# Scores of a sliding-window attention on half blocks: 32 queries by 96 keys in eight parts of the PE array

## The chip, the cores and the metric

One core of a Trainium2 chip runs the kernel. The metric is the device time of one execution in microseconds. Three runs of the kernel before gave 360.49, 361.76 and 361.85 us; the median, 361.76 us, is the time before. PE is the matrix engine (its matmuls; PEld is its weight loads), DVE the vector engine, ACT the scalar engine, POOL the general engine, and SP's queue issues the transfers.

## The reference

A causal attention with a window of 64 positions, then a gated feed-forward layer. Eight batches, eight heads, 576 positions, 64 features a head; all in 32-bit floats.

```python
scores = scale * np.matmul(q, k.transpose(0, 1, 3, 2))
rel = pos[:, None] - pos[None, :]
mask = (rel >= 0) & (rel < window)          # window = 64
scores = np.where(mask, scores, -1000000000.0)
attn = np.exp(scores - np.max(scores, axis=-1, keepdims=True))
attn = attn / (np.sum(attn, axis=-1, keepdims=True) + 1e-09)
x = np.matmul(attn, v)                       # heads side by side: (8, 576, 512)
for k in range(5):                           # gate_pre: a causal convolution of five taps
    gate_pre += conv_w[k][None, None, :] * xp[:, k:k + S, :]
gate = 1.0 / (1.0 + np.exp(-gate_pre))
out = (gate * (x @ w_val)) @ w_out
```

The two weights and the convolution's words come as 64-bit floats and are split on the chip into two 32-bit parts.

## The kernel before, in words

**Attention.** The 576 positions of a head are 9 blocks of 64 queries. A block needs 128 keys: its own 64 and the 64 before it. Heads go in pairs (tile index hh, 0 or 1; a pair has 128 features on the partitions, 64 each), which makes 32 pairs and 288 blocks. Blocks are worked off in 36 groups m of eight blocks. A group has one score tile per head in PSUM, 128 partitions by 4 by 128 keys: four times two blocks on top of each other. The steps of a group, with the names that the code gives them:

- S(m), L433: 16 products, 64 queries by 128 keys each, on quarters of the array (64 rows by 64 columns: the head chooses the rows, the place of the block in the tile the columns). A product of 32-bit floats is two matmuls in the trace, so a group has 32.
- M(m,hh), L452: on DVE, four operations that add a mask tile and take the row minimum of the negated scores (`nm`); X(m,hh), L464: on ACT, four exponentials that also sum (`su`).
- Ra, Rb (L469 POOL, L474 DVE): the sums and their reciprocals `rc`. N(m,hh): the product with them, on POOL as one operation (L486) or on ACT as four (L484).
- PT(m,hh), L493: four transposes on PE into one PSUM bank (tile `pt`, one buffer); EP, L201: ACT copies them out (`pts`).
- AV(i), L516: for a pair i, 18 products with the values into PSUM (tile `av`).
- XH, XL: the result is split into a rounded part `xh` and a rest `xl` (ACT or DVE, then DVE).

**Convolution.** Five taps of a pair. The letter of the pair in `conv` chooses the way: K means taps as products with diagonal matrices `dg` on PE (L574, tile `g`, from a copy `x` of the result, step EX) and a copy out of PSUM (CC); P, and every pair behind the string, means one tap on ACT (L607) and four on DVE (L609). Before, three pairs of batch 0 went by PE. SIG, L804, is the sigmoid of a batch on ACT; batch 0's was in two pieces (`gate`), and each return from sigmoid to exponential loads a table.

**Feed-forward.** Per batch eight V pieces of 12 matmuls (L647, 288 columns), then HF on DVE (product with the gate), HH on ACT and HL on POOL (its split into `h_hi` and `h_lo`), and output tiles O of 12 matmuls (L713, 512 columns), EO (copy out) and a store.

**What sets the order.** Nothing is moved by hand. Each step is an `Op` with a cost per engine, what it depends on, what buffers it takes and frees, and a priority (`prio` plus the offset of its kind in `off`). `in_order` is a list planner: it plays the program through with these costs, and at each point takes for each engine the ready step that can start first. What comes out is written to each engine's queue in that order, and every engine runs its queue strictly in order. V, O and HF carry a large priority number (`ffn_prio`), so that they fill in where attention cannot go on. In the first microseconds, where PE would wait, the loop at the end puts spare products of the identity (L827) into PE's queue, as many as the planned gap holds.

The array has three shapes: whole (V, O, PT, taps), quarters (S) and halves by columns (AV). The planner charges `drain` for a change between them.

## Time and profile before

| | |
|---|---|
| median of three runs | 361.76 us (360.49 to 361.85) |
| profiled execution | 361.33 us, its span 359.5 us |
| PE busy | 351.7 us, 3994 matmuls |
| ACT busy | 286.9 us |
| DVE busy | 257.4 us |
| POOL busy | 129.3 us |
| transfers | 52.08 MB, 145 GB/s in the mean |
| granted PE clock | full in all slices |

The busy time of PE is a union over matmuls that overlap, and their ends are modelled, so it tells that something of PE is under way and not how full the array is. Lengths of pieces in the chain of waits are from the start of a piece to the start of what follows it there, and can be added. A group's busy time counts overlapping instructions once, its mean is that of one.

### The profile page before, as it was taken

Reading aid. Unit: us, or ns where it says so; the run is one execution under the profiler, and the core shown is the slowest. Engines: PE = TensorE matmul, PEld = TensorE weight load, DVE = VectorE, ACT = ScalarE, POOL = GpSimd, SP = SyncE. Lnnn points to the kernel's source line nnn. Section 1 sums busy time; section 2 is a strip of 40 time slices with the busy share of each in tenths; the row PEclk is TensorE's granted clock in tenths of the full one; section 3 lists DMA queues with packets and bytes.
Section 4 is the critical chain, followed back from the end, with each engine's and each line's share of the span. In section 5 each row is a group of like instructions: output and inputs, shape, how many; then the busy total and the mean of one; then the engine's idle time right before and its main releaser. Section 6 shows DMA issues by size and latency. Waiting matters only on the chain.

```text
span 359.5 us, 10642 instructions
## 1 busy us (share of the span) xinstructions
PE 351.7 (98%) x3994; PEld 310.1 (86%) x3994; DVE 257.4 (72%) x927; ACT 286.9 (80%) x929; POOL 129.3 (36%) x197
## 2 busy tenths in 40 slices
PE   8999999989999999999999999999999999999996
PEld 7888778978899878998899888997899888988985
DVE  4999999997587588887788866786888773672300
ACT  2988999999999999997999988998899854333222
POOL 7141545373145622451244612443244400330510
PEclk9999999999999999999999999999999999999999
DMA  8984474254573335445544455345422241002012
GB/s 275 397 328 133 142 234 130 95 198 162 193 228 133 100 125 190 133 133 176 180 162 133 134 190 192 123 146 173 143 62 84 86 150 66 0 32 88 2 58 88
DMA packets 22291, 52.08 MB, mean 145 GB/s; under 512 B 2656, under 2 KB 4960, under 8 KB 22240
## 3 DMA queue, kind: packets, MB, share of 16 engines
q1 hardware_dynamic: 22240, 51.41, 42.4%
q8 instruction: 31, 0.51, 0.6%
q14 instruction: 20, 0.16, 0.1%
HBM read 41.96 MB, written 9.44 MB: 143 GB/s over the span
## 4 chain that ended last, share of the span: by engine, by line
PE 69%; ACT 18%; DVE 9%; DMA 1%; issue 1%; POOL 0%; DVEq 0%; ACTq 0%
PE o L713 26%; PE v L647 20%; ACT p L464 8%; PE av L516 8%; PE s L433 6%; PE pt L493 6%; DVE gp L609 3%; PE g L574 3%; DVE p L452 2%; ACT pts L201 2%; ACT p L484 1%; ACT h_hi L201 1%; ACT gp L607 1%; ACT L464 1%; DMA st<-in_w_val_dram 1%
## 5 line engine op out<-in xcount | busy, mean ns | idle before, releaser
L464 ACT ACTIVATE p<-p,nm 128x128 f32<-128x128 f32 x288 | 112.5, 399 | 2.3 <-DVE nm L452 2.1
L609 DVE SCALAR_TENSOR_TENSOR gp<-av,cw,gp 128x575 f32<-128x575 f32 (+1 forms) x116 | 94.1, 811 | 7.8 <-ACT gp L607 6.5
L676 POOL TENSOR_TENSOR h_lo<-hf,h_hi 128x288 fp32r<-128x288 f32 (+2 forms) x80 | 53.7, 683 | 99.4 <-ACT h_hi L201 98.3
L647 PE MATMUL v<-xl,wv_hi 128*128 128x288 f32 x256 | 78.6, 307 | 0.0
L647 PE MATMUL v<-xh,wv_hi 128*128 128x288 f32 x256 | 75.4, 295 | 0.0
L647 PE MATMUL v<-xh,wv_lo 128*128 128x288 f32 x256 | 75.4, 295 | 0.0
L452 DVE CUSTOM_DVE_ANT_0 p<-s,mask 128x128 f32<-128x128 f32 x288 | 65.2, 284 | 12.7 <-PE s L433 12.0
L713 PE MATMUL o<-wo_hi,h_lo 128*128 128x512 f32 (+1 forms) x148 | 60.2, 406 | 1.1 <-POOL h_lo L676 1.1
L713 PE MATMUL o<-wo_lo,h_hi 128*128 128x512 f32 (+1 forms) x148 | 57.8, 391 | 0.0
L486 POOL TENSOR_TENSOR p<-p,rc 128x512 f32<-128x512 f32 x49 | 51.4, 1061 | 17.8 <-DVE rc L474 16.5
L713 PE MATMUL o<-wo_hi,h_hi 128*128 128x512 f32 (+1 forms) x148 | 57.5, 389 | 0.0
L464 ACT ACTIVATION_READ_ACCUMULATOR p<-p,nm 128x1 f32 x288 | 56.6, 196 | 0.0
L647 PEld LDWEIGHTS v<-xl,wv_hi 128*128 128x128 f32 x256 | 48.1, 188 | 2.1 <-issue 1.7
L647 PEld LDWEIGHTS v<-xh,wv_hi 128*128 128x128 f32 x256 | 48.2, 188 | 0.1
L647 PEld LDWEIGHTS v<-xh,wv_lo 128*128 128x128 f32 x256 | 48.1, 188 | 0.0
L493 PE MATMUL pt<-ident,p 128*128 128x128 f32 x288 | 44.2, 276 | 1.8 <-ACT pts L201 1.6
L201 ACT CAST h_hi<-hf 128x288 fp32r<-128x288 f32 (+2 forms) x80 | 28.5, 383 | 19.0 <-DVE hf L658 18.8
L469 POOL TENSOR_SCALAR su<-su 128x8 f32<-128x8 f32 x36 | 9.9, 275 | 93.8 <-ACT p L464 93.6
L201 ACT COPY pts<-pt 128x512 f32<-128x512 f32 x72 | 41.9, 583 | 1.8 <-PE pt L493 1.5
L658 DVE TENSOR_TENSOR hf<-v,gp 128x288 f32<-128x288 f32 x64 | 29.0, 454 | 19.1 <-PE v L647 18.3
L516 PEld LDWEIGHTS av<-pts,v 128*64 128x64 f32 x1152 | 36.2, 138 | 6.4 <-issue 3.5
L493 PEld LDWEIGHTS pt<-ident,p 128*128 128x128 f32 x288 | 33.8, 140 | 8.4 <-issue 3.1
(122 smaller groups left out, 506.8 us busy)
## 6 DMA issues: line engine op xcount, KB each, us to landing
v<-in_vw_dram SPq DMA_DIRECT2D x32, 576.0 KB, 4.2
out_dram<-ot SPq DMA_DIRECT2D x35, 256.0 KB, 2.0
qtb<-in_qT_dram SPq DMA_DIRECT2D x31, 288.0 KB, 4.4
ktb<-in_kT_dram SPq DMA_DIRECT2D x31, 288.0 KB, 4.6
st<-in_w_val_dram SPq DMA_DIRECT2D x4, 512.0 KB, 7.6
st<-in_w_out_dram SPq DMA_DIRECT2D x2, 1024.0 KB, 10.0
qtb<-in_qT_dram SPq DMA_DIRECT2D x1, 256.0 KB, 3.7
ktb<-in_kT_dram SPq DMA_DIRECT2D x1, 256.0 KB, 5.0
```

What stands on the lines that cost most here:

```text
L201: nc.scalar.copy(out=out, in_=in_)
L433: nc.tensor.matmul(sp_t[m, hh][half * W:half * W + W, t, :], lhsT=held("qt", i)[r, j * W:j * W + W], rhs=held("kt", i)[r, j * W:j * W + P] ...
L452: nc.vector.tensor_tensor_reduce(out=pe[:, t, :], in0=sp_t[u][:, t, :], in1=mk[first], scale=-SCALE, scalar=3.0e38, op0=ALU.add, op1=ALU.m ...
L464: nc.scalar.activation(out=pe[:, t, :], in_=pe[:, t, :], func=AF.Exp, scale=-1.0, bias=nm[:, t:t + 1], accum_out=su[:, t:t + 1])
L486: MUL[e](out=pe, in0=pe, in1=rc.unsqueeze(2).broadcast_to([P, GB, P]))
L493: nc.tensor.transpose(out=tp[:, t, :], in_=pe[:, t, :], identity=ident)
L516: nc.tensor.matmul(ap[hh * D:(hh + 1) * D, j * W:(j + 1) * W], lhsT=v_t[i][:, hh * NB + j, :], rhs=pts_t[m, hh][:, t, half * W:(half + 1) ...
L609: nc.vector.scalar_tensor_tensor(out=acc, in0=x, scalar=col, in1=acc, op0=ALU.mult, op1=ALU.add)
L647: nc.tensor.matmul(vp_t[u][:, 0:NH], lhsT=w[:, c, js], rhs=x[:, c, hs], start=(a + z == 0), stop=(a + z == NM - 1))
L658: nc.vector.tensor_mul(out=hf, in0=vp_t.pop(u)[:, 0:NH], in1=gp_t[b][:, jb, hs])
L676: SUB[e](out=h_lo[:, jb, dst:dst + hi - lo], in0=hf_t[u][:, lo:hi], in1=h_hi[:, jb, dst:dst + hi - lo].bitcast(F32))
L713: nc.tensor.matmul(op_t[key][:, 0:cs.stop - cs.start], lhsT=h[:, jb, col:col + P], rhs=w[:, jb, cs], start=(a + z == 0), stop=(a + z == NM ...
```

## The change

Scores are taken on half blocks: 32 queries need only 96 keys, so a group has 32 products of 32 queries by 96 keys. They lie on eight parts of the array, 64 rows by 32 columns (`tile_position`); four blocks stand on top of each other in a score tile, and the four positions along it are two blocks by two halves. Mask, row minimum and exponential work on 96 columns; nine mask tiles of 96 columns replace three of 128. The probabilities lie at the first 96 columns for first halves and at the last 96 for second halves of eight fixed tiles `pb`, whose other 32 columns are set to zero once, so that transposes and AV keep their shape. AV reads the 64 queries of a block as two runs of 32.

Around it: pair 1 leaves the way by PE (`conv` KKKP becomes KPKP), each tap on PE is a step of its own that the planner can place, the first step of the weights' split may go to ACT as an absolute value, N may go to DVE, batch 0's sigmoid is one piece, v has two buffers and hf four, the planner chooses by rank among the steps that can start within `look` of the first, and single steps have offsets of their own (`adj`). Spares are written into a free bank of the taps once such a bank was used.

```diff
...
-    sb={'p': 8, 'pts': 6, 'v': 3, 'qt': 3, 'kt': 3, 'ot': 2, 'hf': 3, 'w': 2, 'x': 2},
+    sb={'p': 8, 'pts': 6, 'v': 2, 'qt': 3, 'kt': 3, 'ot': 2, 'hf': 4, 'w': 2, 'x': 2},
-    flex=dict(EP='A', EO='AV', HH='A', XH='AV', HL='G', CC='AV', N='GA', EX='AV', WR='GV', DG='V'),
+    flex=dict(EP='A', EO='AV', HH='A', XH='AV', HL='G', CC='AV', N='GVA', EX='A', WR='GV', DG='GV', WH='AV'),
-    gate={0: (0, 2, 4)},
+    gate={},
-    conv='KKKP',
+    conv='KPKP',
+    adj={'PT(6, 1)': -7.65, 'PT(4, 1)': -2.76, 'EP(1, 1)': -0.17, 'X(6, 1)': -1.73,
...
+    look={'A': 100, 'P': 0, 'G': 450, 'V': 0},
...
                     continue
                 k = (t - (CFG["wait"] if e == "P" and op.prio < CFG["ffn_prio"] else 0)
                      - (CFG["stay"] if e == "P" and "F" != mode and op.mode != "F" else 0), op.rank)
-                if pick is None or k < pick[0]:
-                    pick = (k, op)
+                cand.append((k, op))
+            if cand:
+                limit = min(k for k, _ in cand)[0] + CFG["look"].get(e, 0)
+                pick = min((c_ for c_ in cand if c_[0][0] <= limit), key=lambda c_: c_[0][1])
             if pick and (best is None or pick[0] < best[0]):
                 best = (pick[0], e, pick[1])
         if best is None:
...
+    Q, KW = W // 2, W + W // 2
     mk = {}
...
+    def mask(where_):
+        m32 = const.tile([P, KW], F32, name="mask" if where_ is None else "mask%d%d" % where_)
+        if where_ is None:
+            nc.gpsimd.memset(m32, 0.0)
+            for c in range(4):
+                r = slice(c * Q, c * Q + Q)
+                nc.gpsimd.affine_select(
+                    out=m32[r], in_=m32[r], pattern=[[1, KW]], compare_op=ALU.is_ge,
+                    fill=NEG / SCALE, base=-1, channel_multiplier=-1)
+                nc.gpsimd.affine_select(
+                    out=m32[r], in_=m32[r], pattern=[[-1, KW]], compare_op=ALU.is_ge,
+                    fill=NEG / SCALE, base=W, channel_multiplier=1)
+        else:
+            c, par = where_
+            nc.gpsimd.tensor_copy(out=m32, in_=mk[None])
+            nc.gpsimd.memset(m32[c * Q:c * Q + Q, 0:W - par * Q], NEG / SCALE)
+        mk[where_] = m32
+    for where_ in [None] + [(c, par) for c in range(4) for par in range(2)]:
+        mask(where_)
+    pb = [const.tile([P, GB, P], F32, name=f"pb{i}") for i in range(SB["p"])]
+    for t in pb:
+        nc.vector.memset(t[:, 0:2, KW:P], 0.0)
+        nc.vector.memset(t[:, 2:4, 0:P - KW], 0.0)
...
+        def head(e):
             w2 = words().rearrange("p (n t) -> p n t", t=2)
             t["low"], t["high"] = w2[:, :, 0], w2[:, :, 1]
             for x in "aml":
                 t[x] = sb(tag + x, [P, n], f"{name}{x}", I32, bufs=SB.get(tag, 1))[0:rows]
                 t[x + "f"] = t[x].bitcast(F32)
-            ts(out=t["m"], in0=t["high"], scalar1=0x7FFFFFFF, scalar2=None, op0=ALU.bitwise_and)
+            if e == "A":
+                nc.scalar.activation(out=t["mf"], in_=t["high"].bitcast(F32), func=AF.Abs)
+            else:
+                ts(out=t["m"], in0=t["high"], scalar1=0x7FFFFFFF, scalar2=None, op0=ALU.bitwise_and)
         def clamp(_):
...
     def scores(m):
-        ss = (2 * m, 2 * m + 1)
-        prio = ss[0] * GB * PB
-        at = [where(s, t) for s in ss for t in range(GB)]
+        prio = 2 * m * GB * PB
+        at = [where(8 * m + n) for n in range(8)]
         last = [i for i, j in at if j == NB - 1]
         def e_s(_):
             for hh in range(2):
                 sp_t[m, hh] = ps("s", [P, GB, P], f"s{m}_{hh}")
             for t in range(GB):
-                for half, s in enumerate(ss):
-                    i, j = where(s, t)
+                par, tt = divmod(t, 2)
+                for c in range(4):
+                    i, j = at[4 * tt + c]
+                    q0 = j * W + par * Q
                     for hh in range(2):
                         r = slice(hh * D, hh * D + D)
-                        nc.tensor.matmul(sp_t[m, hh][half * W:half * W + W, t, :],
-                                         lhsT=held("qt", i)[r, j * W:j * W + W],
-                                         rhs=held("kt", i)[r, j * W:j * W + P], start=True, stop=True)
+                        nc.tensor.matmul(sp_t[m, hh][c * Q:c * Q + Q, t, 0:KW],
+                                         lhsT=held("qt", i)[r, q0:q0 + Q],
+                                         rhs=held("kt", i)[r, q0:q0 + KW], start=True, stop=True,
+                                         tile_position=(hh * D, c * Q))
             for i in last:
                 give("qt", i)
                 give("kt", i)
-        so = prev["S"] = op(f"S{m}", ("P", 227 * GB), e_s,
+        so = prev["S"] = op(f"S{m}", ("P", 172 * GB), e_s,
                             list({id(o): o for o in map(lq_of.get, at)}.values()) + [prev.get("S")], take=[("ps_s", (m, 0)), ("ps_s", (m, 1))],
                             free=[(k, i) for i in last for k in ("qt", "kt")], prio=prio, mode="Q")
         done, xs = [], []
+        keys = [slice(t // 2 * (P - KW), t // 2 * (P - KW) + KW) for t in range(GB)]
         for hh in range(2):
             u = (m, hh)
             def e_m(_, u=u):
                 nm = nm_t[u] = sb("nm", [P, GB], f"nm{u[0]}_{u[1]}", bufs=SB["p"])
-                pe = p_t[u] = sb("p", [P, GB, P], f"p{u[0]}_{u[1]}")
+                pe = p_t[u] = take("p", u)
                 for t in range(GB):
-                    first = tuple(where(s, t)[1] == 0 for s in ss)
+                    par, tt = divmod(t, 2)
+                    first = [(c, par) for c in range(4) if at[4 * tt + c][1] == 0]
                     nc.vector.tensor_tensor_reduce(
-                        out=pe[:, t, :], in0=sp_t[u][:, t, :], in1=mk[first],
+                        out=pe[:, t, keys[t]], in0=sp_t[u][:, t, 0:KW], in1=mk[first[0] if first else None],
                         scale=-SCALE, scalar=3.0e38, op0=ALU.add, op1=ALU.min,
                         accum_out=nm[:, t:t + 1])
-            mo = op(f"M{u}", ("V", 210 * GB), e_m, [so], take=[("p", u)], free=[("ps_s", u)], prio=prio)
+            mo = op(f"M{u}", ("V", 178 * GB), e_m, [so], take=[("p", u)], free=[("ps_s", u)], prio=prio)
...
-                    nc.scalar.activation(out=pe[:, t, :], in_=pe[:, t, :], func=AF.Exp, scale=-1.0,
+                    nc.scalar.activation(out=pe[:, t, keys[t]], in_=pe[:, t, keys[t]], func=AF.Exp, scale=-1.0,
                                          bias=nm[:, t:t + 1], accum_out=su[:, t:t + 1])
-            xs.append(op(f"X{u}", ("A", 386 * GB), e_x, [mo] + xs, prio=prio))
+            xs.append(op(f"X{u}", ("A", 359 * GB), e_x, [mo] + xs, prio=prio))
         def e_r1(_):
...
-                s, t = divmod(i * NB + j, GB)
-                m, half = divmod(s, 2)
+                m, n = divmod(i * NB + j, 8)
+                tt, c = divmod(n, 4)
                 for hh in range(2):
                     nc.tensor.matmul(ap[hh * D:(hh + 1) * D, j * W:(j + 1) * W],
                                      lhsT=v_t[i][:, hh * NB + j, :],
-                                     rhs=pts_t[m, hh][:, t, half * W:(half + 1) * W], start=True, stop=True)
+                                     rhs=pts_t[m, hh][:, tt::2, c * Q:c * Q + Q], start=True, stop=True)
             del v_t[i]
             for m in done:
...
             end = 0 if way == "K" else 1
+            done = [xl_o]
             for half in range(2):
-                def e_cv(_, half=half):
-                    g = gc_t[i, half] = ps("f", [P, 512], f"g{i}_{half}")
-                    for kk in range(TAPS - 1, end - 1, -1):
+                cv = None
+                for kk in range(TAPS - 1, end - 1, -1):
+                    def e_cv(_, half=half, kk=kk):
                         back = TAPS - 1 - kk
+                        if back == 0:
+                            gc_t[i, half] = ps("f", [P, 512], f"g{i}_{half}")
                         lo = back if half == 0 else 0
-                        nc.tensor.matmul(g[:, lo:NH], lhsT=dg[:, (hp * TAPS + kk) * P:(hp * TAPS + kk + 1) * P],
+                        nc.tensor.matmul(gc_t[i, half][:, lo:NH], lhsT=dg[:, (hp * TAPS + kk) * P:(hp * TAPS + kk + 1) * P],
                                          rhs=x_t[i][:, half * NH + lo - back:half * NH + NH - back],
                                          start=back == 0, stop=kk == end)
-                cv = op(f"K{i}_{half}", ("P", 500 * (TAPS - end)), e_cv, [ex, dgo[hp]], take=[("ps_f", (i, half))],
-                        free=[("x", i)] if half and not end else [], prio=cp)
+                    cv = op(f"K{i}_{half}_{kk}", ("P", 500), e_cv, [ex, dgo[hp], cv],
+                            take=[("ps_f", (i, half))] if kk == TAPS - 1 else [], prio=cp)
                 def e_cc(e, half=half):
...
-    spare = ps("f", [P, P], "spare")
+    spare = [(ps("f", [P, 512], "spare"), 0.0)]
     since, until, margin, each = CFG["awake"]
-    at = since
+    at, freed, opened = since, {}, {}
     for o in order:
         if o.engine == "P":
-            if any(kind == "ps_f" for kind, _ in o.take):
+            if o.name.startswith("V"):
                 until = 0
             if o.start < until:
-                for _ in range(int((o.start - at - margin) // each)):
-                    nc.tensor.matmul(spare, lhsT=ident, rhs=ident, start=True, stop=True)
+                t_ = next((t for key, t in reversed(opened.items()) if freed.get(key, 1e9) < at), None)
+                if not opened:
+                    t_ = spare[0][0]
+                for _ in range(int((o.start - at - margin) // each) if t_ is not None else 0):
+                    nc.tensor.matmul(t_[:, 0:P], lhsT=ident, rhs=ident, start=True, stop=True)
...
```

The order that comes out differs in most places. Two of them follow. The first is on PE in the first third of batch 0, from the end of a group of scores over the transposes of a group (`pt`) to the taps (`g`). Before:

```order
L433 MATMUL s_0_490<-ktb_74,qtb_71 64x128
L433 MATMUL s_1_491<-ktb_74,qtb_71 64x128
L493 MATMUL pt_1_515<-ident,p_1_389 128x128 x4
L574 MATMUL g_0_523<-x_486,dg 128x288
L574 MATMUL g_0_523<-x_486,dg 128x287
L574 MATMUL g_0_523<-x_486,dg 128x286
L574 MATMUL g_0_523<-x_486,dg 128x285
L574 MATMUL g_0_523<-x_486,dg 128x284
L574 MATMUL g_1_551<-x_486,dg 128x288 x5
L516 MATMUL av_568<-pts_0_412,v_144 64x64
```

And of the change:

```order
L463 MATMUL s_0_555<-ktb_74,qtb_71 32x96
L463 MATMUL s_1_556<-ktb_74,qtb_71 32x96
L528 MATMUL pt_0_594<-ident,pb_135 128x128 x4
L871 MATMUL spare<-ident 128x128
L612 MATMUL g_1_613<-x_602,dg 128x288
L528 MATMUL pt_1_622<-ident,pb_134 128x128 x4
L612 MATMUL g_1_613<-x_602,dg 128x288 x2
L463 MATMUL s_0_637<-ktb_74,qtb_71 32x96
L463 MATMUL s_1_638<-ktb_74,qtb_71 32x96
```

The ten taps of a pair stood together; now they are dealt out between transposes, scores and AV, the second half of the positions first, and the scores have the new form. In all PE's order has 60 tap rows in the trace's count before and 40 now, and 150 spare matmuls instead of 130.

The second is the head of ACT's queue, from the first cast of a weight (`wv_hi`) over the first exponentials (`p` or `pb` with `su`) to the first copies of transposes (`pts`). Before:

```order
L380 CAST wv_hi<-w0a 128x4x128
L464 ACTIVATE p_0_200,su_215<-p_0_200,nm_0_199 128x128 x4
L464 ACTIVATE p_1_209,su_215<-p_1_209,nm_1_208 128x128 x4
L380 CAST ch<-cwa 128x20
L380 CAST wv_hi<-w2a 128x4x128
L484 ACTIVATE p_0_200<-p_0_200,rc_281 128x128 x4
L464 ACTIVATE p_0_287,su_304<-p_0_287,nm_0_286 128x128 x4
L201 COPY pts_0_326<-pt_0_315 128x512
L464 ACTIVATE p_1_298,su_304<-p_1_298,nm_1_297 128x128 x4
L201 COPY pts_1_344<-pt_1_337 128x512
L484 ACTIVATE p_0_287<-p_0_287,rc_371 128x128 x4
```

And of the change, from the row behind that cast:

```order
L497 ACTIVATE pb_130,su_259<-pb_130,nm_0_245 128x96 x4
L377 ACTIVATE cwm<-cwords 128x20
L497 ACTIVATE pb_131,su_259<-pb_131,nm_1_254 128x96 x4
L408 CAST ch<-cwa 128x20
L408 CAST wv_hi<-w2a 128x4x128
L517 ACTIVATE pb_130<-pb_130,rc_342 128x96 x4
L497 ACTIVATE pb_133,su_374<-pb_133,nm_0_356 128x96 x4
L211 COPY pts_0_382<-pt_0_368 128x512
L377 ACTIVATE w1m<-st_168 128x512
L497 ACTIVATE pb_132,su_374<-pb_132,nm_1_345 128x96 x4
L211 COPY pts_1_444<-pt_1_394 128x512
L408 CAST wv_hi<-w1a 128x4x128
```

The heads of the split (L377: `cwm` from the convolution's words, `w1m` from w_val) have moved from DVE's queue into ACT's, between the exponentials, and the cast of w1, which stood 36 rows into ACT's queue, now stands behind group 1's exponentials.

Later in the program the order of kinds is much the same, batch by batch; one difference is that the output tile of row 1024 stood ahead of group 16's first transposes and now stands behind them and behind AV of pair 12.

83 lines of the change are left out of this document (43 added, 40 removed).

## The prediction

> **What bounds the kernel now.** I read three views: the busy sums, ACT alone in three stages, and the chain that ended last in order of time. First the sums, which say little by themselves:
>
> ```profile
> PE 351.7 (98%) x3994; PEld 310.1 (86%) x3994; DVE 257.4 (72%) x927; ACT 286.9 (80%) x929; POOL 129.3 (36%) x197
> ```
>
> Whether PE is really full is seen from the lengths of its pieces in the chain (start, length, what):
>
> ```profile
> 29.13 4.84 PE g L574 x20
> 33.96 1.20 PE av L516 x36
> 35.16 1.03 PE s L433 x32
> ...
> 318.17 11.44 PE o L713 x48
> 329.60 12.75 PE v L647 x96
> 342.35 14.07 PE o L713 x72
> ```
>
> and from the counts of its groups:
>
> ```profile
> L493 PE MATMUL pt<-ident,p 128*128 128x128 f32 x288 | 44.2, 276 | 1.8 <-ACT pts L201 1.6
> L516 PE MATMUL av<-pts,v 128*64 128x64 f32 x1152 | 40.6, 225 | 0.3 <-DVE gp L609 0.2
> L433 PE MATMUL s<-ktb,qtb 64*64 64x128 f32 x1152 | 40.1, 275 | 0.1
> L827 PE MATMUL spare<-ident 128*128 128x128 f32 x130 | 18.7, 302 | 1.5 <-POOL ident masks.py:199 1.5
> ```
>
> and from where PE starts:
>
> ```profile
> 1.45 5.34 PE L827 MATMUL spare<-ident 128*128 128x128 f32 x26 [1.45 <-POOL ident masks.py:199]
> ```
>
> A tap takes 4.84 / 20 = 0.242 us for 288 columns, 0.84 ns a column. Added up: 36 groups of scores x 1.03 = 37.1; 32 AV x 1.20 = 38.4; 60 taps x 0.242 = 14.5; 64 V pieces x 12.75 / 8 = 102.0; the output tiles, 36 in all with two halves, x 14.07 / 5 = 101.3; 288 transposes and 130 spares at 128 x 0.84 = 0.1075 each, 31.0 and 14.0. That is 338 us out of the 355 from the first spare (1.45) to 356.4. The 17 left are the changes of array shape between pieces and short waits. So PE has no slack to hide anything in: what is taken off it counts, as far as its suppliers follow.
>
> The supplier that may not follow is ACT (length of the window, ACT busy):
>
> ```profile
> 0.00:56.50 56.50, 45.45 (x160) 1.00 0.73 252
> 56.50:147.20 90.70, 90.03 (x314) 1.00 0.47 157
> 147.20:318.00 170.80, 139.96 (x434) 1.00 0.38 124
> ```
>
> From 56.5 to 147.2, where the copy of group 16's first transposes ends, ACT idles 0.67 us. There both engines are full at once; behind 147 ACT idles 31 us and only PE is left.
>
> **The change, part by part.**
>
> *Scores.* A group of scores had 16 products of 128 columns, each as two matmuls (1152 = 36 x 32), on four parts of the array. One part alone would need 32 x 0.1075 = 3.44 us; the row shows 1.03, so four run at a time: 8 rounds x 0.1075 = 0.86, and 0.17 to fill and drain. Now there are 32 products of 96 columns, 64 matmuls, on eight parts. If eight run at a time, that is again 8 rounds, of 96 x 0.84 = 0.0806: 0.645 + 0.17, and some 0.025 for issuing eight instead of four into the first round, 0.84 us. The saving is 0.19 x 36 = 6.9 us. No row of before has four column parts with one set of rows, so both sides are bounded. Upper: nothing is saved if the rounds stay 0.107. Worst: four of the eight run, 16 rounds x 0.0806 + 0.17 = 1.46 us, 15.5 us lost. The weight loads decide between these ends:
>
> ```profile
> L647 PEld LDWEIGHTS v<-xh,wv_hi 128*128 128x128 f32 x256 | 48.2, 188 | 0.1
> L516 PEld LDWEIGHTS av<-pts,v 128*64 128x64 f32 x1152 | 36.2, 138 | 6.4 <-issue 3.5 <-DVE gp L609 0.8 <-DVE nm L452 0.5
> L433 PEld LDWEIGHTS s<-ktb,qtb 64*64 64x64 f32 x1152 | 31.3, 132 | 4.4 <-issue 2.3 <-DVE nm L452 0.2 <-DVE wv_lo L386 0.2
> ```
>
> 64 columns more take 188 - 138 = 50 ns. AV has two column parts over all rows, 18 rounds in 1.20 us, 67 ns each; two loads of 64 columns in turn would take 100. So loads into different columns overlap, and I take 0.84.
>
> [...]
>
> AV now reads its 64 queries as two runs of 32, the same columns at the same price.
>
> *Taps.* The table goes from three K in batch 0 to two: 20 of 60 matmuls go, 20 x 0.242 = 4.8 us of PE. In their place DVE gets four taps of some 0.7 us.
>
> *Spares.* The order has 150 instead of 130: 20 x 0.1075 = 2.15 us more on PE.
>
> *PE's sum:* -6.9 - 4.8 + 2.15 = -9.5 us.
>
> *ACT up to the same copy (group 16, first head).* The order gives the counts, these rows the prices:
>
> ```profile
> 68.97 1.55 ACT p L464 x8
> 70.53 1.17 ACT p L484 x4
> 51.69 0.54 ACT xh L201
> 53.77 0.64 ACT gp L607
> 20.14 0.51 ACT wo_hi L380
> 98.16 0.47 ACT ot L201
> ```
>
> ```profile
> L201 ACT COPY pts<-pt 128x512 f32<-128x512 f32 x72 | 41.9, 583 | 1.8 <-PE pt L493 1.5
> L201 ACT COPY gp<-g 128x288 f32<-128x288 f32 x4 | 1.6, 392 | 0.4 <-PE g L574 0.3
> L804 ACT ACT_TABLE_LOAD x8 | 10.3, 1283 | 2.2 <-DVE gp L609 2.1
> ```
>
> A column costs (583 - 392) / 224 = 0.85 ns, 32 columns 27 ns; of four instructions, 0.11. Forty exponentials: -4.4. Normalisations 13 x 1.17 become 12 x 1.06: -2.5. Table loads 8 to 6 (batch 0's sigmoid is one piece now): -2.6. Heads of the weights by absolute value, four of 0.51 and a small one: +2.3. Three more casts of xh: +1.6; a first tap: +0.6; three output copies: +1.4; two copies of g less: -0.6. Sum: -4.2.
>
> PE by then: 20 groups of scores x 0.19 = 3.8, taps 4.8, spares -2.15, and the output tile of row 1024, which stood ahead of these transposes and now stands behind (2.81): 9.3 us earlier. So ACT is 9.3 - 4.2 = 5.1 us late for PE's new pace, unless it idles less at the start. Its idle there, 11.05 us, by releaser:
>
> ```profile
> L464 ACT ACTIVATE p<-p,nm 128x128 f32<-128x128 f32 x57 | 22.2, 392 | 1.8 <-DVE nm L452 1.7
> L201 ACT COPY pts<-pt 128x512 f32<-128x512 f32 x11 | 6.3, 573 | 1.3 <-PE pt L493 1.0
> L484 ACT ACTIVATE p<-p,rc 128x128 f32<-128x128 f32 x16 | 5.1, 390 | 1.1 <-DVE rc L474 1.1
> ```
>
> Up to group 5's reciprocal DVE's list gets shorter by some 8 us: two of three casts of xh, one of three steps of dg, weight heads and rests move or come later, and 56 maxima lose 32 columns at about 1.04 ns (a column of 754 - 454 over 288):
>
> ```profile
> L204 DVE CAST xh<-av 128x576 fp32r<-128x576 f32 x19 | 14.3, 754 | 10.0 <-PE av L516 9.8
> L204 DVE COPY gp<-g 128x288 f32<-128x288 f32 x2 | 0.9, 454 | 0.0
> ```
>
> So most of the 4.2 us should go. Against it stand two new waits in ACT's queue: a head that waits for the convolution's words with an exponential behind it, and the cast of w1, which waits for five steps on DVE. I take 3 us won, between 0 and 4.2. PE is then held by 5.1 - 3 = 2.1 us.
>
> *At nothing:* the masks. POOL has eight selections for twelve, but eight copies and eight fills more. The first maximum needs two of these and started when the scores came:
>
> ```profile
> 4.24 0.54 DVE L351 TENSOR_SCALAR w0m<-st 128x512 int32<-128x512 int32 x1 [3.14 <-DMA st<-in_w_val_dram]
> 4.56 2.02 POOL L234 TENSOR_SCALAR_AFFINE_SELECT mask<-mask 64x128 f32<-64x128 f32 x4
> 6.63 0.54 POOL L238 MEMSET mask<- 64x64 f32 x2
> 8.17 0.29 DVE L452 CUSTOM_DVE_ANT_0 p<-s,mask 128x128 f32<-128x128 f32 x1 [0.56 <-PE s L433]
> ```
>
> Selections of 0.4 us saved and copies of 0.2 (a fill of this size) to 0.5 (half of a 512-column product) put them at 6.7 to 9.1: 0 to 1 us late, taken as nothing. DVE's sixteen fills of about 0.1 us lie in its wait of 3.14 us for w_val. Two buffers of v instead of three: a load lands in 4.2 us and 32 AV share 355 us, one every 11.
>
> ```profile
> v<-in_vw_dram SPq DMA_DIRECT2D x32, 576.0 KB, 4.2
> ```
>
> **Sum.** The profiled execution took 361.3 (span 359.5 and 1.8 around it): 361.3 - 9.5 + 2.1 = 353.9. Some single transposes now stand beside each other or beside AV, with fewer drains; for that, and 0.4 by which the median of the runs lies above this execution, I forecast 353.5.
>
> **Rivals.**
>
> *ACT holds PE fully.* Its early waits only change place. For it: 90.03 of 90.70. Against: DVE's shorter list. 361.3 - 9.5 + 5.1 = 357.
>
> *The rounds stay at 0.107*, by the loads in turn. Only -4.8 + 2.15 is left, and ACT, 4.2 us earlier, follows: 361.3 - 2.7, 359 as a median. AV's rounds speak against it.
>
> *The scores get slower.* Four column parts of a row group read four streams of keys from the same 64 partitions; until now two do. If that read is the limit, the eight go in two halves: 1.46 us a group, 15.5 - 2.7 = 12.9 more, 374. It decides from 1.10 us a group on. For it: in no row do more than two parts read one set of rows. Against: in AV two column parts and their loads cost nothing beside each other. [...]
>
> *The change is made but the order takes it back:* spares into a tap's own bank must wait for DVE's copy of it, with AV and scores of batch 0 queued behind. Under 1 us; it stays inside the range.
>
> **How the numbers follow.** Forecast 0.67; ACT holds 0.14; rounds unchanged 0.11; slower scores 0.08. A measurement of this kernel tells 0.5%, 1.8 us, from no change. The forecast's own range is 350.5 to 356; with ACT's case and about half of the unchanged rounds it is 349.5 to 359, and 374 is left out. Faster: nearly all of the first two and half of the third, 0.85; same 0.06; slower 0.09.
>
> **What would show it.** Right: the chain's scores x64 at 0.80 to 0.87 us; weight loads of 32 columns near 110 ns; ACT still over 98% busy from 56 on but until about 143; taps x40. The copy of group 16 comes at 138 to 143. Wrong: scores at 1.0 or above; PE pieces that wait for pts or nm in the second hundred us; first maximum behind 8.6.

## The result and the profile after

Five runs of the changed kernel gave a median of **355.77 us** (355.68 to 355.93), five runs of the kernel before on the same chip 361.61 (360.49 to 361.85). The ratio is 0.9846 with a 95% interval of 0.9829 to 0.9862: 1.5% faster. The forecast was 353.5 with a range of 349.5 to 359.0. The profiled execution has a span of 354.0 us instead of 359.5. One of the eight runs of the kernel with 20 taps more, below, took 558.34 us at a granted clock of 0.559 and is left out there.

The busy sums of the changed kernel, and its group of exponentials:

```profile
PE 345.5 (98%) x5146; PEld 305.2 (86%) x5146; DVE 240.7 (68%) x926; ACT 280.1 (79%) x936; POOL 136.0 (38%) x210
...
L497 ACT ACTIVATE pb<-pb,nm 128x96 f32<-128x96 f32 x288 | 104.5, 371 | 2.2 <-DVE nm L485 2.2
```

PE is as full as before, with 1152 matmuls more (the scores) and 6.2 us less busy time. An exponential over 96 columns takes 371 ns; the mean over the same 288 was 399 before, and 27 ns less were worked out.

The chain of waits of the changed kernel shows the new pieces (start, length, what):

```profile
30.61 0.93 PE s L463 x54
...
48.55 2.42 PE g L612 x10
```

A group of scores takes **0.93 us**, against 1.03 before and 0.84 forecast (the chain names some 55 of its 64 matmuls; the trace has them all, 2304 in 36 groups). A tap is still 0.242 us. The line of the scores by itself (durations in ns, least, median and most):

```profile
L463 PEld LDWEIGHTS s<-ktb,qtb x2304: 102/106/108, 6.5 to 267.5; 64*32 64x32 f32 x192
L463 PE MATMUL s<-ktb,qtb x2304: 239/243/268, 6.5 to 267.6; 64*32 64x96 f32 x192
```

ACT alone, in the windows of the prediction and up to the end of group 16's copy, which now comes at 141.2 us instead of 147.1 (length, ACT busy):

```profile
0.00:56.50 56.50, 49.35 (x193) 1.00 0.74 255
56.50:143.00 86.50, 83.48 (x287) 1.00 0.49 159
...
0.00:141.20 141.20, 131.06 (x475) 1.00 0.59 198
```

Before, the same work up to 147.1 was

```profile
0.00:147.10 147.10, 135.38 (x473) 1.00 0.57 193
```

So ACT does 4.3 us less up to that point and idles 10.1 us instead of 11.7. Of these two effects the copy is 5.9 us earlier; the whole span is 5.5 us shorter.

**Where the time came from.** I added up PE's list of each kernel, the time that its pieces need one behind the other, from the order and the measured length of each piece. This is an estimate: 349.7 us before, 342.1 after. From the start of a group of scores to the next piece it is 1.034 us before and 0.927 after, so the scores give 36 x 0.107 = 3.9 less; taps give 4.7 less, spares 2.2 more, transposes that stand beside other work of their shape or beside each other 1.1 less (in the chain of the changed kernel four of them take 0.59 us between scores and taps, at 47.96 us, and 0.47 between taps, at 50.97), the rest 0.1 less: together 7.6. The span fell by 5.5. The difference, 2.1 us, is by this sum time in which PE waits longer than before. The profile's own measure, span minus busy time, has only 0.7 us more of it (7.8, then 8.5), so the 2.1 is not known to better than some 1.4 us. Behind the first microseconds, PE's waits of over 0.4 us in the changed kernel all lie before 70 us.

### The profile page after: what moved, and what is told of

Read it like the earlier page. It is cut to its first block, busy times and chain, and to the rows that moved or that the text cites. A ratio compares the mean times of both kernels' runs of the same rounds, so it can differ in the third digit from the quotient of the medians.

```text
span 354.0 us, 12956 instructions
## 1 busy us (share of the span) xinstructions
PE 345.5 (98%) x5146; PEld 305.2 (86%) x5146; DVE 240.7 (68%) x926; ACT 280.1 (79%) x936; POOL 136.0 (38%) x210
## 4 chain that ended last, share of the span: by engine, by line
PE 78%; ACT 11%; DVE 5%; DMA 4%; issue 1%; SPq 0%; POOL 0%; ACTq 0%; DVEq 0%
PE o L754 27%; PE v L688 24%; PE av L551 9%; PE pt L528 8%; PE s L463 7%; ACT pb L497 4%; DMA st<-in_w_val_dram 3%; PE g L612 2%; ACT pts L211 2%; DVE gp L650 1%; DVE pb L485 1%; DMA ktb<-in_kT_dram 1%; ACT pb L517 1%; ACT L497 1%; DVE xl L584 1%
## 5 line engine op out<-in xcount | busy, mean ns | idle before, releaser
L650 DVE SCALAR_TENSOR_TENSOR gp<-av,cw,gp 128x575 f32<-128x575 f32 (+1 forms) x120 | 97.3, 811 | 14.6 <-ACT gp L648 13.1
L497 ACT ACTIVATE pb<-pb,nm 128x96 f32<-128x96 f32 x288 | 104.5, 371 | 2.2 <-DVE nm L485 2.2
L485 DVE CUSTOM_DVE_ANT_0 pb<-s,mask 128x96 f32<-128x96 f32 x288 | 55.6, 251 | 16.6 <-PE s L463 13.7
L520 POOL TENSOR_TENSOR pb<-pb,rc 128x512 f32<-128x512 f32 x50 | 52.5, 1063 | 19.2 <-DVE rc L507 15.8
L497 ACT ACTIVATION_READ_ACCUMULATOR pb<-pb,nm 128x1 f32 x288 | 56.1, 195 | 0.0
L528 PE MATMUL pt<-ident,pb 128*128 128x128 f32 x288 | 44.3, 276 | 2.9 <-ACT pts L211 2.5
L528 PEld LDWEIGHTS pt<-ident,pb 128*128 128x128 f32 x288 | 33.6, 140 | 10.3 <-ACT pts L211 4.3
L551 PE MATMUL av<-pts,v 128*64 128x64 f32 x1152 | 40.6, 225 | 0.4 <-DVE gp L650 0.2
```

The source lines that it names most:

```text
L485: nc.vector.tensor_tensor_reduce(out=pe[:, t, keys[t]], in0=sp_t[u][:, t, 0:KW], in1=mk[first[0] if first else None], scale=-SCALE, scalar ...
L497: nc.scalar.activation(out=pe[:, t, keys[t]], in_=pe[:, t, keys[t]], func=AF.Exp, scale=-1.0, bias=nm[:, t:t + 1], accum_out=su[:, t:t + 1])
L520: MUL[e](out=pe, in0=pe, in1=rc.unsqueeze(2).broadcast_to([P, GB, P]))
L528: nc.tensor.transpose(out=tp[:, t, :], in_=pe[:, t, :], identity=ident)
L551: nc.tensor.matmul(ap[hh * D:(hh + 1) * D, j * W:(j + 1) * W], lhsT=v_t[i][:, hh * NB + j, :], rhs=pts_t[m, hh][:, tt::2, c * Q:c * Q + Q] ...
L650: nc.vector.scalar_tensor_tensor(out=acc, in0=x, scalar=col, in1=acc, op0=ALU.mult, op1=ALU.add)
```

## The experiments

Every run had the kernel before beside it on the same chip; its medians there were 361.2 to 361.6 us, so that the times below can be set against 355.8 for the changed kernel.

### One half of the change at a time

*The new order with the old scores.* In the changed kernel the scores were put back to 64 queries by 128 keys, and with them the width of masks, maxima, exponentials and normalisations. The table of numbers that sets the order, and the order itself, are those of the change.

```diff
-            for t in range(GB):
-                par, tt = divmod(t, 2)
-                for c in range(4):
-                    ... [c * Q:c * Q + Q, t, 0:KW], lhsT 32 columns, rhs 96 columns
+            for t in range(GB):
+                for half in range(2):
+                    ... [half * W:half * W + W, t, :], lhsT 64 columns, rhs 128 columns
```

> The changed kernel's order on every engine, but the work of the scores as before: 64 queries by 128 keys on quarters of the array, and mask, maximum, exponential and normalisation on 128 columns. My theory: PE's list grows by 36 x 0.104 = 3.7 us, ACT's by 72 x 0.11 for the exponentials and 22 x 0.11 for normalisations, 5.6 us of it up to group 16, where ACT paces; so PE is held by some 3 us more: 362.5 us, and the new order alone brings nothing. Rival, ACT does not pace: 355.8 + 3.7 = 359.5 us, or less.

362.91 us (362.70 to 363.71); ratio to before 1.0056, 1.0036 to 1.0076. The theory holds. PE's list is some 4 us shorter than before, since two thirds of the taps are left, and yet the kernel is 0.6% slower. ACT's part of this kernel, in the windows of above:

```profile
0.00:56.50 56.50, 49.71 (x188) 1.00 0.73 254
56.50:143.00 86.50, 84.85 (x286) 1.00 0.45 145
```

From 56.5 to 143 ACT is 98% busy. The new order by itself is no gain.

*The new scores with the old settings.* The other half: the changed kernel's scores and widths, with before's table (but two buffers of the values, as in the change).

```diff
-    conv='KPKP',
+    conv='KKKP',
-    adj={'PT(6, 1)': -7.65, ...
+    adj={},
-    look={'A': 100, 'P': 0, 'G': 450, 'V': 0},
+    look={'A': 0, 'P': 0, 'G': 0, 'V': 0},
...
```

> The new scores, mask and columns, but the planner's settings of before: its offsets and priorities, three pairs by PE, batch 0's sigmoid in two pieces, heads of the weights on DVE, no look-ahead (two buffers of v as in the change). PE's list, from its order and the lengths of pieces, is 2.8 us longer than in the changed kernel. My theory: 355.8 + 2.8, less up to 1 us since ACT is relieved as in the change: 358 us (357 to 360), so the scores bring some 3.5 of the 5.8 us and the rest comes from the order. Rival, the change lives by its order: 361 us or more.

364.52 us (364.13 to 365.15); ratio 1.0094, 1.0070 to 1.0119. My expectation was wrong, the rival right: new scores without an order made for them make the kernel slower. Its PE list is 344.9 us, 2.8 more than with the change (20 taps more, fewer spares), and its waits are 6.1 us more; together the 8.9 by which its span (362.9) is longer. Half of these waits are one place, between 75 and 82 us. The chain there (start, length, what), in the order of time:

```profile
75.32 0.54 ACT xh L211
75.86 0.02 issue
75.88 0.76 DVE xl L584
...
81.39 1.53 PE s L463 x61
82.92 2.12 PE av L551 x36
```

DVE has two sets of maxima, taps and a step of the weights queued behind one cast; scores wait for the maxima that free their bank; and PE stands for 1.36 us and then, two matmuls into the group, for 2.51. AV's products behind that wait take 2.12 instead of 1.20 us, because the granted clock has fallen to a half (length, PE busy and, behind the count, the mean clock in two windows of this run):

```profile
70.00:84.00 14.00, 10.13 (x280) 0.87 0.44 135
82.90:85.00 2.10, 2.10 (x40) 0.50 0.62 169
```

Together, these two runs say that the 5.8 us are neither the scores' nor the order's: by their ratios, either alone loses 2.0 and 3.4 us.

### What sets the length of a group of scores

*Each group issued twice* (the same 64 products of weights and keys again, into the same places).

```diff
-            for t in range(GB):
+            for t in list(range(GB)) * 2:
                 par, tt = divmod(t, 2)
```

> The changed kernel with every group of scores issued twice, one behind the other (the second time over the first, so the result is unchanged): 128 pairs of weight load and matmul a group instead of 64. In the changed kernel a group takes 0.93 us: its first four rounds start 82 ns apart, then the pairs start 16.7 ns apart whatever the array could take. Theory: PE's sequencer has a stock of some 32 pairs, and behind it pairs arrive every 16.7 ns. Then the second 64 pairs cost 64 x 16.7 = 1.07 us and a group takes 2.0 us; the run takes 355.8 + 36 x 1.07 = 394 us. Rival, the array is slowed evenly by eight parts that read or load at once: 0.76 us for eight rounds, twice that and 0.17 to fill and drain, 1.69 us a group, 383 us.

One run: 406.34 us. An undisturbed group takes 1.66 us, 0.73 for the second 64 pairs, which is 11.4 ns a pair or 91 a round of eight. The length is near the rival's, but neither mechanism fits: the pairs of the second half come 11.4 ns apart in the mean and not 16.7, and the group is not slower throughout, since its first 32 pairs start at the same offsets as in the single group. And the time rose by 50 us where 36 groups x 0.73 account for 26. Most of the rest, 18 us, is time in which PE waited for nothing that the profile shows ("issue"). These are PE's longest waits in that run (us in all, times, the longest); the changed kernel has no wait of PE for issue:

```profile
PE s L463 <- issue: 11.6, 11, 2.4
PE pt L528 <- issue: 4.3, 2, 2.9
PE av L551 <- issue: 2.2, 2, 1.2
```

*The scores of before in pieces of 32 keys* (same four parts of the array and weights of 64 columns, each stream a quarter as long, so four times as many pairs: 128 a group).

```diff
-                        nc.tensor.matmul(sp_t[m, hh][half * W:half * W + W, t, :], lhsT=..., rhs=...[r, j * W:j * W + P])
+                for y in range(0, P, 32):
+                    ...
+                            nc.tensor.matmul(sp_t[m, hh][half * W:half * W + W, t, y:y + 32], lhsT=..., rhs=...[r, j * W + y:j * W + y + 32])
```

> The kernel before with each product of 64 queries by 128 keys issued as four of 64 by 32 (same result): 128 pairs a group on four parts, weight loads of 64 columns instead of 32, the same columns streamed. Theory of the arriving pairs: some 32 at once (0.22 us), 96 x 16.7 = 1.60, 0.17 to fill and drain, 2.0 us a group; 361.6 + 36 x 0.97 = 396 us. Rival, the limit behind the first rounds is the weight loads themselves, by their columns: 33 ns a pair, 3.2 to 4.2 us a group, over 440 us. Rival, four streams reading at once on one set of rows were the limit: only two read here, so a group stays at 1.03 us and the run at 362.

One run: 403.64 us. The chain of this run has whole groups of

```profile
36.30 2.00 PE s L439 x128
44.92 2.00 PE s L439 x128
```

The first theory named the right size for the wrong reason: here there is no break at the 33rd pair; from the second round on four pairs follow every 58 ns, 14.6 ns a pair, from the first to the last. A stream of 32 columns needs only 27 ns (32 x 0.84, from the taps), so the streams do not set this pace; the pairs with 64-column weights come 58 / 2 = 29 ns apart on each set of rows. Four loads one after another, at the 50 ns for 64 columns that the prediction took from the load rows, would be 200 ns a round: that fell. So did the second rival, by which a group would stay at 1.03 us with only two parts reading one set of rows.

*The new scores in pieces of 32 keys* (eight parts, weights of 32 columns, 192 pairs a group).

```diff
-            for t in range(GB):
+            for t, y in [(t, y) for t in range(GB) for y in range(0, KW, 32)]:
...
-                        nc.tensor.matmul(sp_t[m, hh][c * Q:c * Q + Q, t, 0:KW],
+                        nc.tensor.matmul(sp_t[m, hh][c * Q:c * Q + Q, t, y:y + 32],
```

> The changed kernel with each product of 32 queries by 96 keys as three of 32 keys: 192 pairs of weight load and matmul a group on the eight parts, each with a stream of 32 columns (27 ns). It tells why eight matmuls take 95 to 103 ns once a group is under way instead of 81. If PE's supply of pairs sets it (12 ns a pair, as the doubled group ran): 192 x 12 = 2.3 us a group. If the four streams on one set of rows or the loads set it (81 to 103 ns is then a price of columns): a third of that a round, 24 rounds of 30 to 55 ns, 0.9 to 1.4 us. Downstream work is unchanged, so the time rises by 36 times the difference at least: above 400 by the first, 357 to 375 by the second.

One run: 482.89 us. The sum of the time came out as the first case says, but the groups did not. Where a group is not interrupted, its 192 pairs start within 1.63 to 1.66 us. One such group in three stretches (start and end, length, PE busy, matmuls under way in it):

```profile
20.43:20.67 0.24, 0.24 (x32) 1.00 0.90 358
20.67:20.98 0.31, 0.31 (x59) 1.00 0.68 266
20.98:22.09 1.11, 1.11 (x152) 1.00 0.27 107
```

The first row has the first 32 matmuls, the others count those still under way too: 32 pairs in 0.24 us, the next 31 steps in 0.306, and the last 128 in 1.11, 8.7 ns a pair. So PE was given a pair every 8.4 ns here, two by two every 16.7; 12 ns a pair is no limit of the supply. Most groups were interrupted, though. The timeline of one of them:

```profile
26.94 1.11 PEld L463 LDWEIGHTS s<-ktb,qtb 64*32 64x32 f32 x120
29.23 0.74 PEld L463 LDWEIGHTS s<-ktb,qtb 64*32 64x32 f32 x72 [1.18 <-issue]
```

After 120 short pairs without a longer piece between, PE stands for 1.2 us with nothing to wait for that the profile shows. In all it stood like this 25 times inside a row of pairs, all but once after 108 to 181 of them:

```profile
PE s L463 <- issue: 49.6, 25, 4.0
```

Of the 127 us that the run takes more, the uninterrupted groups would make 36 x 0.84 = 30 (1.75 to 1.78 us from the start of a group to the next piece, against 0.93); the rest came with these gaps and others like them in front of other pieces, 65 us in all, and with a mean clock of 0.925.

*64 of the 96 keys* (scores, maxima, exponentials and ACT's normalisations; the other 32 keys are left out).

```diff
-                        nc.tensor.matmul(sp_t[m, hh][c * Q:c * Q + Q, t, 0:KW],
+                        nc.tensor.matmul(sp_t[m, hh][c * Q:c * Q + Q, t, 0:64],
...
-                                         rhs=held("kt", i)[r, q0:q0 + KW], start=True, stop=True,
+                                         rhs=held("kt", i)[r, q0:q0 + 64], start=True, stop=True,
```

> The changed kernel with scores, maxima, exponentials and ACT's normalisations over 64 of the 96 keys (the other 32 are left out): the same 64 weight loads and matmuls a group, streams of 64 columns (54 ns). It tells what the 95 to 103 ns a round is made of once a group is under way. If it is the stream and a fixed 15 to 22 ns behind it: 69 to 76 ns a round, a group of 0.65 to 0.75 us. If it is a supply of some 12 ns a pair: 95 to 103 ns a round still, a group of 0.85 to 0.9 us. With a supply of 8.4 ns a pair (the fastest pace of the thirds) alone: 67 ns a round, 0.6 to 0.65. I expect the first. The time falls by ACT's and PE's shorter work: 348 to 352.

349.57 us (349.49 to 350.22), in the range given. A group takes 0.79 us, between the cases. It is clearer by halves. The first and second 32 matmuls of one group, in this run and then in the changed kernel (the second row counts those still under way from the first):

```profile
29.85:30.12 0.27, 0.27 (x32) 1.00 1.03 406
30.12:30.50 0.38, 0.38 (x60) 1.00 0.81 315
```

```profile
30.54:30.89 0.35, 0.35 (x32) 1.00 0.91 358
30.89:31.30 0.41, 0.41 (x55) 1.00 0.14 51
```

From the first matmul to the 33rd it is 267 ns with 64 keys and 354 with 96: 87 less, and three rounds of 32 columns are 81 to 83. **The first half follows the streams** from 96 to 64 columns; with 32, in the run before, it is 240 ns, only 27 less, so that something else sets it there. From the 33rd to the 64th, three rounds later, it is 375 and 400 ns (306 with 32 keys): 25 less where three rounds would have given 81. **The second half does not.** The starts inside one group of the changed kernel, in ns, show where it changes:

```
first 32:  0 7 14 20 27 34 40 47 | 107 114 ... 154 | 189 196 ... 236 | 272 279 ... 319
last 32:   354 385 402 419 435 437 452 469 485 490 506 519 523 539 556 573 573 589 589 605 606 622 639 655 655 672 672 689 705 721 738 754
```

The second to the fifth round start 82 to 83 ns apart, the eight of a round 6.7 ns. From the 33rd on, a start every 16.7 ns, one at a time at first, two at a time in between, one at a time at the end. What remains open is why the two streams of 16.7 ns run into step only late. Nor does any run here show what sets the break: on eight parts it stands behind the 32nd pair with 32, 64 and 96 keys alike, and on four parts, with 64-column weights, the row of 128 pairs above has no break there.

### Who sets the pace in the first 143 us: ACT?

*Exponentials over 64 of the 96 columns* (32 columns are left as they are).

```diff
+                    few = slice(keys[t].start, keys[t].start + 64)
-                    nc.scalar.activation(out=pe[:, t, keys[t]], in_=pe[:, t, keys[t]], func=AF.Exp, scale=-1.0,
+                    nc.scalar.activation(out=pe[:, t, few], in_=pe[:, t, few], func=AF.Exp, scale=-1.0,
```

> The changed kernel with each exponential over 64 of its 96 columns (one half block of keys is left unexponentiated); order, PE and DVE untouched. Each exponential gets 32 columns x 0.85 ns = 27 ns shorter; 40 passes of four up to group 16's copy make 4.4 us less on ACT there. Theory (ACT holds PE in the first 143 us of the changed kernel by about 2 us more than before, some 5 us of PE's waits there are for ACT): these waits mostly go, 355.8 becomes 352 to 354. Rival (PE's waits there have other causes: the maxima, DVE's steps for the weights, the order of the list): 355.3 to 356.3.

354.80 us (354.66 to 355.08); ratio 0.9825, 0.9810 to 0.9839. That is 1.0 us by the medians and 0.8 by the ratios, between the two: 4.4 us less of ACT's work up to 143 us bring a quarter of that at most. PE's waits for the copies up to 143 us, after and with the shorter exponentials, hardly differ:

```profile
PEld pt L528 <- ACT pts L211: 3.0, 5, 1.1
PE pt L528 <- ACT pts L211: 1.8, 3, 0.9
```

```profile
PEld pt L529 <- ACT pts L211: 2.5, 3, 1.1
PE pt L529 <- ACT pts L211: 1.8, 3, 0.8
```

The rows PEld and PE are the weight loads and the matmuls of the same waits and are not to be added: PE itself waits 1.8 us for these copies, not the 5 that I expected. And part of these waits do not come from ACT's load. Transposes stand right behind those whose copy must free their only bank; the longest of these waits, 1.13 us up to 40.4 us, is 1.09 here and just as long in the runs with fewer spares and with fewer taps, below.

*Exponentials over all 128 columns again* (they then take in 32 columns that belong to no key).

```diff
-                    nc.scalar.activation(out=pe[:, t, keys[t]], in_=pe[:, t, keys[t]], func=AF.Exp, scale=-1.0,
+                    nc.scalar.activation(out=pe[:, t, :], in_=pe[:, t, :], func=AF.Exp, scale=-1.0,
```

> The changed kernel with each exponential over all 128 columns again (the sums and the values then take in 32 columns that belong to no key of these queries); order, PE and DVE untouched. ACT gets 4.4 us more up to group 16's copy, 7.8 us in all. Theory (ACT paces the first 143 us, at 96.5% busy it has 3 us of idle time there): 358 to 360, so the shorter exponentials are worth 2 to 4 us of the change. Rival (PE paces, ACT only fills its own idle time): 355.8 to 356.5.

358.23 us (357.83 to 360.61); ratio 0.9926, 0.9903 to 0.9949. At the lower end of the theory: the exponentials' 32 columns are worth some 2.5 us of the change. The profiled execution (span 358.8) cannot be used to place them, since its second group of scores starts some 3 us late, behind a load of keys that took 9.1 us to land.

### Who sets the pace: PE?

*Fewer spares* (62 instead of 150, none behind the first transposes).

```diff
-            if o.name.startswith("V"):
+            if o.name.startswith(("V", "PT")):
                 until = 0
```

> The changed kernel without its spare matmuls from the first transposes on: 62 instead of 150; PE's list gets 88 x 0.1075 = 9.5 us shorter in the first 45 us. If spares are on the path, as the sum of the prediction took them (+2.15 for 20), the time falls toward 346. If they only fill time in which PE waits anyway: 354.5 to 356, and PE's waits grow by 9 us. Third way: the granted clock falls in the first 60 us without them, and the time rises above 357. I expect the second with ACT as the pace: 354 to 356.

356.34 us (356.07 to 356.51); ratio 0.9866, 0.9849 to 0.9882. PE's list is 9.2 us shorter and the kernel 0.6 us slower, just outside the range that I gave. The clock did fall (three stretches of this run: length, PE busy, and behind the count the mean clock):

```profile
13.50:27.00 13.50, 7.98 (x124) 0.65 0.84 310
17.50:27.70 10.20, 6.67 (x151) 0.50 0.70 260
27.80:36.00 8.20, 8.15 (x217) 1.00 0.81 243
```

From 17.5 to 27.7 us it was a half, and behind that full again. So nothing is won by leaving spares out; whether they only stand where PE waits anyway, as I expected, this run does not show, because a shorter list and a slower clock stand against each other in it.

*One tap of five on PE* (32 of the 40 tap matmuls are left out, so that part of the convolution is not computed).

```diff
-                        nc.tensor.matmul(gc_t[i, half][:, lo:NH], lhsT=...
+                        if back == 0: nc.tensor.matmul(gc_t[i, half][:, lo:NH], lhsT=...
```

> The changed kernel with one of five taps for each half of PE's convolutions (32 of the 40 tap matmuls are left out, so this part of the convolution is not computed); the orders of all other work stay. PE's list gets 32 x 0.25 = 8.2 us shorter up to about 45 us. If PE bounds all through, as the sum's taps term (-4.8 for 20 taps) says: 348. If ACT holds PE in the first 143 us: 353 to 355.5, with more waits of PE for pts. I expect the latter: a shorter PE list in the first 45 us pays less than a third of its length.

357.15 us (355.39 to 357.46); ratio 0.9879, 0.9853 to 0.9904. I expected a small gain, and it is a small loss. The clock fell here too (same columns):

```profile
34.00:54.00 20.00, 16.11 (x404) 0.83 0.65 202
54.00:143.00 89.00, 86.53 (x1479) 1.00 0.48 158
```

PE idles more from 34 to 54 us (16.1 us busy against 18.9 in the changed kernel), its mean clock there is 0.83 (0.50 from 40.1 to 46.8 us), and work at half the clock takes longer (AV 2.12 us for 1.20 in the run with the old settings). But one of the four runs had its full clock, 1.000 where the other three had 0.990, and it took 355.39 us: even so, 8 us less on PE before 54 us win only 0.4. That is one run, without a profile of its own; it speaks for suppliers that hold PE there.

*20 taps more* (one of the two convolutions on PE issues each of its products twice into the same bank, so these taps count twice). This goes the other way, where PE cannot fall idle.

```diff
+                        for again in range(2 if i == 0 else 1):
                             nc.tensor.matmul(gc_t[i, half][:, lo:NH], lhsT=...
-                                         start=back == 0, stop=kk == end)
+                                             start=back == 0 and not again, stop=kk == end and again == (i == 0))
```

> The changed kernel with the products of one of its two kinds of convolution on PE issued twice, each pair behind one another into the same bank (their sums then count those taps twice): as many tap matmuls more, 20, as the change took off, 4.8 us more in PE's list in the first 50 us; all other work and the order stay, and PE does not get idle, so the clock has no reason to fall. If PE paces that stretch, as the sum's taps term (-4.8) says: 360.6. If ACT and DVE pace it (fewer spares and fewer taps brought nothing): PE's waits there, 6 us, swallow most, 356 to 358. I expect the second: 357.5.

**360.25 us** (359.97 to 360.55); ratio 0.9976, 0.9964 to 0.9987. I expected 357.5 and was wrong: 4.8 us of taps cost 4.5. The clock of the profiled execution stayed at 1.000. By the same sum of pieces as above, PE's waits fell by only 0.7 us. The chain of this run at the place, with PE's pieces one behind the other and no wait but one copy of 0.59:

```profile
39.89 1.20 PE g L613 x5
...
42.45 1.16 PE g L613 x4
43.61 0.45 PE pt L528 x4
44.06 0.02 issue
44.08 0.59 ACT pts L211
```

In the changed kernel the chain runs over ACT, POOL and DVE in this stretch, from 34.9 to 45.8 us:

```profile
35.38 2.97 ACT pb L497 x16
...
45.07 0.65 ACT x L211
```

With this, the picture of the two sides is: add 4.8 us to PE's list, and 4.5 is lost; add 4.4 us to ACT's up to 141 us, and 2.5 is lost; take 4.4 from ACT's, and 0.8 to 1.0 is won; take 8 or 9 from PE's, and at most 0.4 is won. I read this as two lists that are nearly level: whichever gets longer sets the pace, and to shorten one alone brings little. PE's waits that are left are mostly short ones in places of their own, which a longer list elsewhere does not fill.

### A truer price for the planner

The planner counted a quarter of a group of scores at 172 ns; the group measures 0.93 us.

```diff
-        so = prev["S"] = op(f"S{m}", ("P", 172 * GB), e_s,
+        so = prev["S"] = op(f"S{m}", ("P", 195 * GB), e_s,
```

> The changed kernel with one number of the planner raised: a quarter of a group of scores at 195 ns instead of 172 (it measured 0.93 us a group). PE's list is as long as before (341.9 for 342.1 us, by the measured pieces), and what differs is which waits it runs into. Theory (the time is PE's list plus waits of 8 to 10 us that an order tuned by its own prices keeps small): 355 to 359, no gain from a truer price. Rival (a truer price brings shorter waits): under 354.

357.61 us (357.20 to 358.01); ratio 0.9891, 0.9874 to 0.9907: 1.8 us slower than the change, with a list as long. The waits moved (one of 1.18 us behind a piece at 73 us, one of 0.98 behind a piece at 196 us, where the change has none). The offsets in the table belong to the prices with which they were found, so a better price alone made this order worse. No kernel of this study that computes everything is faster than the change.

## Why the prediction came out

The time lay 2.3 us above the forecast, just inside its own narrower range (350.5 to 356). By its steps:

- **Scores: the mechanism right, the size off.** -6.9 was forecast, 36 x 0.107 = -3.9 measured; 0.93 us a group lies between the signs for right (0.80 to 0.87) and wrong (1.0). Eight matmuls do run at a time, and the loads of 32 columns take the 106 ns that were to show it. The step that failed is "that is again 8 rounds, of 96 x 0.84 = 0.0806": it holds for the first half of a group (rounds of 82 to 83 ns). In the second four the starts come 16.7 ns apart instead of 6.7, and 31 steps take 400 ns; with a third less columns they take 375. These 3.0 us are the miss; 0.3 came back with the drains (below) and 0.4 because the profiled execution of the changed kernel is its median, where the forecast had added 0.4.
- **Loads in turn** (rounds that stay at 0.107, 359 us). The first four rounds at 82 ns speak against it, and so do 67 ns a round with pieces of 32 keys. At the 50 ns for 64 columns that the prediction took from the load rows, four loads of 32 columns one behind the other would take 100 ns, an estimate; with the same loads both paces are shorter, so the trace disagrees with it. Pairs do have a spacing of their own once a row is under way: with 32-column weights the starts come 16.7 ns apart, two at a time in the rows of 192 pairs, and with 64-column weights four every 58 ns.
- **The slower scores** (374 us, decided from 1.10 us a group on) fell with 0.93. In the first half of each group four parts of one set of rows run beside each other at 82 to 83 ns a round, close to the 81 of a stream by itself (96 x 0.84, from the taps).
- **ACT holds PE fully** (357). By the time alone this rival is the nearer one, 1.2 us off where the forecast is 2.3. Against it: ACT's idle time up to the copy did fall, by 1.6 us, and 4.4 us less on ACT won only 0.8 to 1.0.
- **Spares into a tap's own bank** (under 1 us) cost nothing that shows: PE has no idle time in front of any of the 16.
- **Taps: right.** -4.8 was forecast; 20 taps put back cost 4.5 us of time, and 4.1 of span in the profiled executions.
- **Spares: +2.15 is in the list, but not shown to be on the path.** 88 fewer brought nothing, but with half the clock for 10 us. They and the hold by ACT lie in the same stretch, and part of one may be the other. The sum has 2.15 + 2.1 for the two; the estimate of PE's list has +2.2 and +2.1 in waits, which is the same sum, but no run separates them.
- **ACT's list: right.** -4.2 forecast, 135.38 - 131.06 = 4.3 measured, with group 16's copy at 141.2 (138 to 143 forecast).
- **3 us of early idle won: half right.** In the first 56.5 us ACT's idle fell from 11.05 to 7.15, by 3.9. But behind it ACT is not over 98% busy: 83.48 of 86.50 is 96.5%, and 2.3 us of idle are new there. Up to the copy only 1.6 are won.
- **PE held by 2.1: right in the estimate, by luck.** 7.6 of list against 5.5 of span are 2.1, within the doubt said above. But both numbers that the 2.1 was made of were off, in opposite directions: ACT won 1.6 instead of 3, which alone would make it 3.5, and with the scores at 0.93 PE's list up to that copy shrank by about 1.7 us less than forecast, which takes it back to 1.8. That ACT does the holding is only partly shown: shorter exponentials give back 0.8 to 1.0 us of it. Of the sign for wrong, waits of PE for `pts` in the second hundred us, there are two, 0.6 us in all.
- **At nothing:** the first maximum starts at 7.88 us (8.17 before), so the eight more masks cost nothing, as said, in the row of the timeline:

```profile
7.88 0.25 DVE L485 CUSTOM_DVE_ANT_0 pb<-s,mask 128x96 f32<-128x96 f32 x1
```

- **The drains** (fewer changes of shape beside transposes): 0.8 in the forecast, since 353.9 + 0.4 - 0.8 is 353.5; 1.1 by the estimate.

That the total is right to 0.6% owes something to a list that was complete, and something to luck in the hold.

## What to carry to other kernels

Where one engine's list is full and its suppliers are just behind, test both directions: work put back on the engine showed nearly its full price (4.5 of 4.8 us), while 8 or 9 us taken off won next to nothing (0.4 at full clock, a loss where the clock fell). Narrower streams on the eight parts paid in the first half of a group (354 to 267 ns from 96 to 64 columns) and little in the second (400 to 375); measure one group by its starts, first and last part apart, before multiplying by a column rate. And an order that was found for one set of prices is part of the kernel: here the new scores without their order, and the order without the scores, each lost time, and a truer price in the planner lost 1.8 us.

## What the runs showed of the hardware

- **Eight parts in 32-bit floats** (64 rows by 32 columns each): the first 32 pairs of a group start in rounds that follow each other, behind the first, by 82 to 83 ns with 96 columns and by 56 ns with 64 (75 into the fifth); from the 33rd on the starts come in steps of 16.7 ns, one or two at a time, and 31 steps take 400, 375 and 306 ns with 96, 64 and 32 columns. In long rows with 32 columns they settle at two every 16.7 ns, 8.4 ns a pair. With weights of 64 columns in four parts it is 58 ns for four.
- **In long rows of short pairs PE stood still.** Inside rows of 128 pairs on the eight parts (each group twice) it did so 11 times, in rows of 192 pairs (pieces of 32 keys) 25 times, nearly always after 90 to 181 of them, for 0.2 to 4.0 us and for nothing that the profile shows: 11.6 and 49.6 us in all. In the changed kernel's groups of 64 pairs it did not happen once. What holds the pairs back no run here tests.
- **The granted clock stood at a half where PE idled more:** 0.50 from 17.5 to 27.7 us with fewer spares (PE busy for 6.67 of these 10.2 us) and from 40.1 to 46.8 us with fewer taps, 1.00 before and behind. Over stretches that hold both, PE busy for 8 of 13.5 us came with a mean of 0.65 (fewer spares), 16 of 20 us with 0.83 (fewer taps), 10 of 14 us with 0.87 (old settings); 12.9 of 13.5, in the changed kernel with all its spares, with 1.00 (one row of the same stretch):

```profile
13.50:27.00 13.50, 12.86 (x245) 1.00 0.84 312
```
